# Seven block products in place of eight for some weight pairs of a feed-forward layer, in a fused attention and Fourier-mixing kernel

## The chip, the cores and the metric

The kernel runs on one core of one Trainium2 chip. The metric is the device time of one execution in microseconds (us), given as the median of several runs. One further execution was taken by the hardware profiler; all rows of the profile are from that one.

The engines are named as in the profile: PE (TensorE, matrix products; PEld is its weight load), DVE (VectorE), ACT (ScalarE), POOL (GpSimd) and SP (which here only issues DMAs).

## The reference

For 4 batches, 8 heads, 576 tokens and head size 64, an attention with a learned bias of the relative position gives x (4 x 576 x 512). Then a mixing block follows, all in float32:

```python
X = np.fft.fft(np.fft.fft(x, axis=1), axis=2)
u = x + np.real(X)
un = (u - mean(u)) / np.sqrt(var(u) + 1e-06)        # over the 512 features
ch = np.maximum(un @ w_ch1, 0.0) @ w_ch2            # 512 -> 2048 -> 512
return u + ch
```

The change concerns the product `un @ w_ch1` only.

## The kernel before

**Number format.** Every large product is made from float32r operands. A float32 value is split into a rounded high part and the rest as a low part (`split`: ACT copies the high part, POOL subtracts it to get the low part), and three products high x high, high x low, low x high are summed. `PROD = [(0, 0), (0, 1), (1, 0)]` lists them.

**Stages.** First the bias table is made, then attention runs over 16 units (4 head pairs x 4 batches); its order is written out by hand in the lists `SECOND`, `ORDER` and `TAIL`. The rest is the feed-forward part: four "dense batches" of 512 tokens (four tiles of 128), one for each batch, and a last one of 256 tokens which holds the 64 left-over tokens of all four batches (the "rest").

**A dense batch** (`dense`) runs over 16 feature blocks f of 128 hidden features. For each, `layer(f)` splits the block's first weight `w1[f]` (resident in SBUF, 128 x 512, four blocks of 128 input features), loads and splits the second weight `w2[f]`, makes the hidden features in `up(f)` and applies the ReLU and the split in `relu_parts(f)`. `up(f)` (L956) is 4 input blocks x 3 parts = 12 matmuls that move 512 tokens each. `down(f)` (L981) multiplies the hidden block into four output accumulators, one for each token tile: again 12 matmuls of 512 columns. `down(f-1)` is put behind `layer(f)`. `hps` has two PSUM banks for the results of `up`, `hhp` two buffers for the hidden parts, `wsp` two buffers for each kind of weight part. `end()` (L989) adds the accumulators into x and stores the tiles.

**What runs beside it.** While a batch's dense part runs, the next batch is made ready in small pieces (`prepare`): Fourier mixing (`Mix.pieces`: L652 to L718), mean and variance (L752), and scaling (L776), which writes the token tile `un`. `run` spreads these pieces over the batch's layers by weights written in the code. Then `flip` transposes `un` on PE (`across`, L797), and `high` (ACT, L802) and `low` (DVE, L806) make its two parts `uh` and `ul`, which the next batch's `up` reads. In batch 1, `widen_rest` also converts the last four weight blocks from 64-bit words.

**Order of the instructions.** In the dense part no order is written by hand: the framework lists each engine's instructions by priority (program order) and by its own estimate of when each is ready. Semaphores, buffer reuse and PSUM bank conflicts are handled by the framework.

Of the kernel before, what the change touches and what calls it, by code (L numbers as in the profile page):

```python
# [20 lines left out]
P = 128  # L21
# [109 lines left out]
def body(ctx, tc, a, out):  # L131
# [286 lines left out]
    with ExitStack() as st:  # L418
# [322 lines left out]

        def norm(tiles):
            n = len(tiles)
# [39 lines left out]
        def token_tile(name, n=4):  # L783

            if name not in toks:
                f = pp.tile([P, 2, 2, S], F32, tag="p", name=name, bufs=4)
                toks[name] = f.rearrange("p a b s -> p (a b s)")
            f = toks[name][:, :512 * n].rearrange("p (t d) -> p t d", d=512)
            return f if name == "un" else f.bitcast(F32R)

        def flip(un):
            ut, ps = [], {}

# [13 lines left out]

            return ut, across, high, low

# [3 lines left out]
        tl = [x[:, 0, t] for t in range(4)]  # L813
        un, stats, root, scale = norm(tl)
        ut, across, high, low = flip(un)
        col, w0 = {}, {}

# [75 lines left out]
        for w in TAIL:  # L893
# [12 lines left out]
            else:  # L906
                small[w[0]](*map(int, w[1:]))
        late.close()
        wsp = pool("wsp", 2, stack=st)
        fgp = pool("fgp", 1, stack=st)  # L910
# [16 lines left out]

        def dense(ut, tiles, store, n_first=0, mix=None):
# [6 lines left out]
            hs, w1s, w2s, wfs, hps_ = {}, {}, {}, {}, {}  # L935
            if n_first:
                hps_[0] = w0["ps"]

            def w1_parts(f):
                w1s[f] = split(w1[f], "w1", nc.gpsimd)  # L940

# [27 lines left out]
            def layer(f):  # L969
                if f not in w1s:  # L970
                    w1_parts(f)
# [12 lines left out]

            def end(which=None, parts=1):
# [19 lines left out]
            pieces = []  # L1005
            for f in range(n_first, NF):
# [57 lines left out]
        def prepare(tl, mix=None):  # L1064
# [4 lines left out]
            pcs += [(.65, lambda i=i: scale(i)) for i in range(n)]  # L1069
            ut, across, high, low = flip(un)  # L1070
# [6 lines left out]
            return tl, ut, pcs, [lambda t=t: one_tile(t) for t in range(n)]  # L1077

        rest_tiles = [x[:, 0, 4], x[:, 2, 4]]
        mix = Mix(1)  # L1080
        for b in range(B):
            def store(t, b=b):
                nc.sync.dma_start(out[4 * b + t], x[:, b, t])

            main, last_down, end = dense(ut, tl, store, 0 if b else 2, mix)
            if b + 1 < B:
                tl, ut, pcs, fl = prepare([x[:, b + 1, t] for t in range(4)], mix if b == 0 else Mix(b + 1))
            else:
                tl, ut, pcs, fl = prepare(rest_tiles)
            if b == 0:  # L1090
                run((main, 1.), (pcs, .94), (widen_rest(), .75))
            else:
                run((main, 1.), (pcs, .94))
            run((fl + last_down, 1.))
            end()

# [65 lines left out]
```

## Time and profile before

| what | us |
|---|---|
| median of 3 runs (lowest, highest) | 766.18 (766.15, 766.69) |
| the profiled execution, whole | 766.97 |
| its span, first to last instruction | 765.0 |
| PE busy in the span | 746.4 |
| DVE, ACT, POOL busy | 436.1, 432.1, 340.0 |
| dense batches 2, 3 and 4 together | 282.7 (433.37 to 716.10) |

The span is the time that the rows account for. The 2 us between it and the whole execution lie before the first and behind the last instruction. [...]

### The profile page before, as it was taken

How to read it: one execution, taken by the hardware profiler on the slowest of the kernel's cores; microseconds unless marked ns; L12 is line 12 of the kernel's file. 1: busy time of each engine (PE TensorE's matmuls, PEld its weight loads, DVE VectorE, ACT ScalarE, POOL GpSimd, SP SyncE). 2: the span in 40 equal slices, each digit the busy share in tenths (PEclk: the TensorE clock that was granted, in tenths of full speed). 3: DMA queues.
4: the chain of work that ended last, by engine and by line, in shares of the span. 5: the costliest groups of instructions: out<-in, count | busy, mean ns of one | idle time of the engine just before them, and what ended most of it. 6: DMA issues, size and time to landing. Idle time of an engine off the chain costs nothing.

```text
span 765.0 us, 13167 instructions
## 1 busy us (share of the span) xinstructions
PE 746.4 (98%) x4779; PEld 611.8 (80%) x4779; DVE 436.1 (57%) x958; ACT 432.1 (56%) x887; POOL 340.0 (44%) x291
## 2 busy tenths in 40 slices
PE   5899999999999999999999999999999999999998
PEld 3467887888878888878888888888888888888896
DVE  7997584887687888786665523334325331111443
ACT  7997887788888887843333433333333333333453
POOL 0002654754565654134554444544446444444442
PEclk9999999999999999999999999999999999999999
DMA  8988788679579872464421311113111222112332
GB/s 208 242 220 206 196 241 258 185 199 289 135 192 277 229 240 85 127 229 143 147 60 56 110 42 42 41 42 111 30 45 38 56 72 66 55 42 56 114 98 78
DMA packets 57584, 101.39 MB, mean 133 GB/s; under 512 B 8656, under 2 KB 27728, under 8 KB 56400
## 3 DMA queue, kind: packets, MB, share of 16 engines
q1 hardware_dynamic: 53792, 92.69, 43.2%
q10 hardware_dynamic: 3440, 4.78, 1.9%
q0 software_dynamic: 288, 3.08, 1.1%
q8 instruction: 37, 0.61, 0.3%
q14 instruction: 27, 0.22, 0.1%
HBM read 77.85 MB, written 20.02 MB: 128 GB/s over the span
## 4 chain that ended last, share of the span: by engine, by line
PE 91%; DVE 4%; DMA 2%; ACT 2%; issue 1%; SPq 0%; ACTq 0%; DVEq 0%
PE acc L981 26%; PE hp L956 25%; PE s L275 12%; PE o L475 10%; PE t L454 8%; PE bps L404 2%; PE zp L672 2%; PE abp L692 2%; DMA bias<-ring 1%; DVE hd L384 1%; PE t L444 1%; PE ut L797 1%; PE t L506 1%; DMA qT<-qT 1%; ACT ring L350 1%
## 5 line engine op out<-in xcount | busy, mean ns | idle before, releaser
L965 DVE SCALAR_TENSOR_TENSOR hl<-hp,hh 128x512 fp32r<-128x512 f32 (+1 forms) x80 | 51.0, 637 | 198.0 <-ACT hh L964 197.6
L925 POOL TENSOR_TENSOR w1l<-w,w1h 128x512 fp32r<-128x512 f32 x79 | 102.6, 1299 | 109.4 <-ACT w1h L924 107.1
L925 POOL TENSOR_TENSOR w2l<-w2f,w2h 128x512 fp32r<-128x512 f32 x64 | 84.8, 1325 | 106.9 <-ACT w2h L924 106.3
L296 DVE CUSTOM_DVE_ANT_0 p<-s,bias 128x576 f32<-128x576 f32 x128 | 95.2, 753 | 56.1 <-PE s L275 51.3
L956 PE MATMUL hp<-uh,w1l 128*128 128x512 f32 (+1 forms) x316 | 116.1, 368 | 0.0
L956 PE MATMUL hp<-uh,w1h 128*128 128x512 f32 (+1 forms) x316 | 116.0, 368 | 0.0
L924 ACT ACTIVATE w1h<-w 128x512 fp32r<-128x512 f32 x79 | 49.8, 631 | 114.2 <-PE hp L956 108.1
L956 PE MATMUL hp<-ul,w1h 128*128 128x512 f32 (+1 forms) x316 | 114.2, 368 | 0.0
L981 PE MATMUL acc<-w2h,hh 128*128 128x512 f32 x288 | 112.6, 392 | 0.0
L981 PE MATMUL acc<-w2l,hh 128*128 128x512 f32 x288 | 112.3, 390 | 0.0
L924 ACT ACTIVATE w2h<-w2f 128x512 fp32r<-128x512 f32 x80 | 50.5, 631 | 104.9 <-POOL w1l L925 54.6
L981 PE MATMUL acc<-w2h,hl 128*128 128x512 f32 x288 | 107.9, 391 | 0.0
L275 PE MATMUL s<-kh,qs 128*128 128x288 f32 (+1 forms) x320 | 98.3, 326 | 2.8 <-DVE nm L296 2.8
L434 ACT ACTIVATE pt<-t 128x512 f32<-128x512 f32 x141 | 77.8, 595 | 38.5 <-PE t L454 20.7
L311 ACT ACTIVATE p<-p,nm 128x576 f32<-128x576 f32 x128 | 98.2, 772 | 2.3 <-DVE nm L296 2.3
L275 PE MATMUL s<-kl,qs 128*128 128x288 f32 (+1 forms) x320 | 88.3, 295 | 0.9 <-DVE kl L216 0.9
L475 PE MATMUL o<-pt,v 128*64 128x288 f32 x640 | 84.2, 411 | 0.0
L212 POOL TENSOR_SCALAR kh<-kT 128x576 fp32r<-128x576 f32 (+1 forms) x28 | 21.0, 769 | 136.4 <-PE s L275 120.6
L454 PE MATMUL t<-ident,p 128*128 128x128 f32 x576 | 78.8, 273 | 0.6 <-ACT pt L434 0.6
L275 PEld LDWEIGHTS s<-kh,qs 128*128 128x128 f32 (+1 forms) x320 | 58.5, 183 | 19.1 <-issue 7.5
L475 PEld LDWEIGHTS o<-pt,v 128*64 128x64 f32 x640 | 43.3, 137 | 30.8 <-issue 4.7
L956 PEld LDWEIGHTS hp<-uh,w1h 128*128 128x128 f32 x316 | 59.5, 188 | 10.3
(154 smaller groups left out, 1391.6 us busy)
## 6 DMA issues: line engine op xcount, KB each, us to landing
w2f<-w_d SPq DMA_DIRECT2D x80, 256.0 KB, 2.7
raw<-m SPq DMA_DIRECT2D x24, 512.0 KB, 4.5
kT<-kT SPq DMA_DIRECT2D x32, 304.0 KB, 4.8
qT<-qT SPq DMA_DIRECT2D x32, 288.0 KB, 4.4
bias_d<-ring SPq DMA_DIRECT2D x54, 144.0 KB, 2.8
bias<-bias_d SPq DMA_DIRECT2D x24, 288.0 KB, 4.9
v<-v SPq DMA_DIRECT2D x16, 320.0 KB, 5.3
w_d<-wf SPq DMA_DIRECT2D x16, 256.0 KB, 3.5
```

What stands on the lines that cost most here:

```text
L212: nc.gpsimd.tensor_scalar(dst[:, c], src[:, c], 1.0, 0.0, ALU.mult, ALU.add)
L275: nc.tensor.matmul(ps[:m, c, :CH], qs[:, c0:c0 + m], kk[:, k0 + c * CH:k0 + (c + 1) * CH], start=k == 0, stop=k == 1, skip_group_check=True)
L296: nc.vector.tensor_tensor_reduce(p, bank.pop((n, i))[:, :, :CH], bias, -0.125, 3.0e38, ALU.add, ALU.min, nms[n][:, blk:blk + 1])
L311: nc.scalar.activation(p, p, AF.Exp, bias=nms[n][:, blk:blk + 1], scale=-1.0, accum_out=sums[n][:, blk:blk + 1])
L434: nc.scalar.activation(dst, src, AF.Copy)
L454: nc.tensor.transpose(tp[:, 128 * t:128 * t + 128], pb[t].rearrange("p h s -> p (h s)")[:, k0:k0 + 128], ident)
L475: nc.tensor.matmul(os_[u][e, c, :CH], vt[u][:, j, e], pts[u][:, 2 * j + h if j < 4 else 8, c * CH:(c + 1) * CH], start=j == 0, stop=j == 4 ...
L924: nc.scalar.activation(h, src, AF.Copy)
L925: eng.tensor_tensor(l, src, h.bitcast(F32), ALU.subtract)
L956: nc.tensor.matmul(ps[:, :N], w[wi][:, P * kb:P * kb + P], ut[ui][:, kb, :N], start=i == 0, stop=i == len(mm) - 1)
L965: nc.vector.scalar_tensor_tensor(hl[:, :N], ps[:, :N], 0.0, hh[:, :N].bitcast(F32), ALU.max, ALU.subtract)
L981: nc.tensor.matmul(acc[t], h[i][:, P * t:P * t + P], w[j], start=f == 0 and k == 0, stop=f == NF - 1 and k == 2)
```

## The change

For the last three pairs of feature blocks in dense batch 2, the last three in batch 3 and the last six in batch 4 (`START = [0, 5, 5, 2]`, 12 pairs in all), `up(2i)` and `up(2i+1)` are replaced by `pair(i)`. The pair is seen as a 2 x 2 block product: two feature blocks x two halves of the input features, times two halves of the input features x two halves of the tokens (256 each). Eight block products become seven, in the form with sums made ahead on both sides. Each is `product`: 2 input blocks x 3 parts = 6 matmuls that move 256 tokens. The remaining steps:

- `sums_(i)` makes four weight sums on DVE (128 x 256 each), `sum_parts` splits them, `own_parts` splits the plain blocks that are still needed.
- `keep` (ACT) writes the transposed tokens back in float32, into the tile that held the untransposed ones; `token_sums` makes four differences of them (DVE, in place) and splits them. It runs at a batch's begin.
- `one`, `two` and `three` issue 3 + 3 + 1 products and between them five additions of 128 x 256 on DVE and a copy on ACT. A pair takes both banks of `hps`.
- `paired` gives the order of a pair, with `down(f-2)` behind `one`, `down(f-1)` behind `two`, and the next pair's sums between. From the first pair of a batch to the end of that batch PE's order is as written.
- In these batches the preparation of the next one is spread over the layers before the first pair only (10, 10 and 4 layers).
- The normalised tokens of a following batch go to the tile named `raw`, which `widen_rest` also uses in batch 1.
- `dynamic_dma_scratch_size=4096` shrinks the SBUF area for the DMA descriptors that POOL makes; a new pool `sump` of 12 KB in each partition holds the sums' parts.

```diff
-                    un.append(token_tile("un", n))
+                    un.append(token_tile(name, n))
...
+            def keep(t):
+                nc.scalar.activation(un[0][:, t].rearrange("p (k c) -> p k c", c=P), ps[t], AF.Copy)
+            def token_sums():
+                b11, b12, b21, b22 = (un[0][:, i:i + 2, j:j + 256] for j in (0, 256) for i in (0, 2))
+                steps = [(b11, b12, b11), (b12, b22, b12), (b22, b22, b11), (b21, b21, b22)]
+                ts.append(token_tile("th"))
+                ts.append([rp.tile([P, 2, 512], F32R, tag="raw", name="tl") for rp in (rawp, rawd)])
+                def part(k, i, low):
+                    c = slice(256 * i, 256 * i + 256)
+                    src = un[0][:, 2 * i:2 * i + 2, 256 * k:256 * k + 256].rearrange("p t (k c) -> p t k c", c=P)
+                    h, l = (w.rearrange("p k (t c) -> p t k c", c=P) for w in (ts[0][:, 2 * k:2 * k + 2, c], ts[1][k][:, :, c]))
+                    if low:
+                        nc.vector.tensor_tensor(l, src, h.bitcast(F32), ALU.subtract)
+                    else:
+                        nc.scalar.activation(h, src, AF.Copy)
+                res = [(.8, lambda st=st: nc.vector.tensor_tensor(*st, ALU.subtract)) for st in steps]
+                res += [(.1, lambda w=w: part(*w, False)) for w in ((0, 0), (0, 1), (1, 1), (1, 0))]
+                return res + [(.9, lambda w=w: part(*w, True)) for w in ((0, 0), (0, 1), (1, 1), (1, 0))]
+            return ut, across, high, low, (ts, keep, token_sums)
...
+        def sums_(i):
+            f, g = w1[2 * i], w1[2 * i + 1]
+            sx, sy = (rp.tile([P, 512], F32, tag="wf", name="sum") for rp in (rawp, rawd))
+            for dst, one, two, op in (
+                    (sx[:, 0:256], g[:, 0:256], g[:, 256:512], ALU.add),
+                    (sx[:, 256:512], sx[:, 0:256], f[:, 0:256], ALU.subtract),
+                    (sy[:, 0:256], f[:, 0:256], g[:, 0:256], ALU.subtract),
+                    (sy[:, 256:512], f[:, 256:512], sx[:, 256:512], ALU.subtract)):
+                nc.vector.tensor_tensor(dst, one, two, op)
+            ss[i] = [sx, sy]
+        def sum_parts(i, k):
+            src = ss[i][k]
+            h = sump.tile([P, 512], F32R, tag=f"s{k}h", name=f"s{k}h")
+            l = sump.tile([P, 512], F32R, tag=f"s{k}l", name=f"s{k}l")
+            nc.scalar.activation(h, src, AF.Copy)
+            nc.gpsimd.tensor_tensor(l, src, h.bitcast(F32), ALU.subtract)
+            ss[i][k] = h, l
...
+        def own_parts(i):
+            w1_parts(2 * i)
+            src = w1[2 * i + 1][:, 256:512]
+            h = sump.tile([P, 256], F32R, tag="gh", name="gh")
+            l = sump.tile([P, 256], F32R, tag="gl", name="gl")
+            nc.scalar.activation(h, src, AF.Copy)
+            nc.gpsimd.tensor_tensor(l, src, h.bitcast(F32), ALU.subtract)
+            ss[i].append((h, l))
...
+            def product(dst, w, c0, block, first=False):
+                where, k, i = block
+                for kk in range(2):
+                    for wi, ui in PROD:
+                        if where == "u":
+                            src = ut[ui][:, 2 * k + kk]
+                        else:
+                            src = ts[1][k][:, kk] if ui else ts[0][:, 2 * k + kk]
+                        nc.tensor.matmul(
+                            dst, w[wi][:, c0 + P * kk:c0 + P * kk + P], src[:, 256 * i:256 * i + 256],
+                            start=first and kk == wi == ui == 0, stop=kk == 1 and wi == 1, skip_group_check=True)
+            def pair(i):
+                f, hold = 2 * i, {}
+                def one():
+                    x_, (sx, sy, g) = w1s.pop(f), ss.pop(i)
+                    pa, pb = (hps.tile([P, 512], F32, tag="h", name="hp") for _ in range(2))
+                    hold["w"] = x_, sy, g
+                    hold["p"] = pa, pb
+                    product(pa[:, 0:256], x_, 0, ("u", 0, 0), True)
+                    product(pa[:, 256:512], sx, 0, ("t", 0, 0))
+                    product(pb[:, 0:256], sx, 256, ("t", 1, 1), True)
+                    c = hold["c"] = sump.tile([P, 512], F32, tag="c", name="c")
+                    u2 = hold["u"] = toks["raw"][:, 2048:2304]
+                    nc.scalar.activation(c[:, 0:256], pa[:, 0:256], AF.Copy)
+                    nc.vector.tensor_tensor(c[:, 256:512], pa[:, 256:512], c[:, 0:256], ALU.add)
+                    nc.vector.tensor_tensor(u2, pb[:, 0:256], c[:, 0:256], ALU.add)
+                def two():
+                    (x_, sy, g), (pa, pb), c = hold["w"], hold["p"], hold["c"]
+                    product(pb[:, 0:256], sy, 0, ("t", 0, 1))
+                    product(pa[:, 0:256], x_, 256, ("u", 1, 0))
+                    product(pa[:, 256:512], sy, 256, ("u", 1, 1))
+                    nc.vector.tensor_tensor(c[:, 256:512], pb[:, 0:256], c[:, 256:512], ALU.add)
+                    nc.vector.tensor_tensor(pa[:, 256:512], pa[:, 256:512], hold["u"], ALU.add)
+                    hps_[f] = pa
+                    relu_parts(f)
+                def three():
+                    (x_, sy, g), (pa, pb), c = hold["w"], hold["p"], hold["c"]
+                    product(pb[:, 0:256], g, 0, ("t", 1, 0))
+                    nc.vector.tensor_tensor(c[:, 0:256], pb[:, 0:256], c[:, 0:256], ALU.add)
+                    hps_[f + 1] = c
+                    relu_parts(f + 1)
+                return one, two, three
+            def paired(p0):
+                res = []
+                for i in range(p0, NF // 2):
+                    f, (one, two, three) = 2 * i, pair(i)
+                    more = [(w1_parts, 0), (w1_parts, 1)]
+                    if i + 1 < NF // 2:
+                        more = [(sums_, i + 1), (sum_parts0, i + 1), (own_parts, i + 1), (sum_parts1, i + 1)]
+                    more = [(lambda m=m: m[0](m[1])) for m in more]
+                    res += [one] + more[:-3] + [lambda f=f: down(f - 2), lambda f=f: (w2_load(f), w2_parts(f)), two]
+                    res += more[-3:-2] + [lambda f=f: down(f - 1), lambda f=f: (w2_load(f + 1), w2_parts(f + 1))]
+                    res += more[-2:-1] + [three] + more[-1:]
+                return res
...
                 pieces.append(lambda f=f: layer(f))
-                if 0 < f < NF - 1:
+                if 0 < f < (2 * p0 if p0 else NF) - 1:
                     pieces.append(lambda f=f: down(f - 1))
+            if p0:
+                pieces = pieces, paired(p0)
...
+                if n == 4:
+                    keep(t)
...
+        START = [0, 5, 5, 2]
...
+            main, last_down, end = dense(ut, tl, store, 0 if b else 2, mix, ts, START[b])
+            first = token_sums() if b else []
...
+                run((fl + last_down, 1.))
+                end()
+                continue
+            i = START[b]
+            first = [(1.7, lambda: sums_(i)), (.1, lambda: sum_parts0(i)), (.1, lambda: sum_parts1(i))] + first
+            first += pcs + [(.1, lambda: own_parts(i))]
+            run((main[0], 1.), (first, .96))
+            with tc.manual_schedule(engines={PE_}):
+                for piece in main[1] + fl[:2] + last_down[:1] + fl[2:] + last_down[1:]:
+                    piece()
+                end()
...
-    nc = bacc.Bacc("TRN2", target_bir_lowering=False, num_devices=1)
+    nc = bacc.Bacc("TRN2", target_bir_lowering=False, num_devices=1, dynamic_dma_scratch_size=4096)
```

## Rows read from the trace of the kernel before

**Rows 1.** The page: span, busy time by engine, slices of the span.

```profile
span 765.0 us, 13167 instructions
PE 746.4 (98%) x4779; PEld 611.8 (80%) x4779; DVE 436.1 (57%) x958; ACT 432.1 (56%) x887; POOL 340.0 (44%) x291
PEclk9999999999999999999999999999999999999999
```

**Rows 2.** The page: the chain that ended last, by engine and line.

```profile
PE 91%; DVE 4%; DMA 2%; ACT 2%; issue 1%; SPq 0%; ACTq 0%; DVEq 0%
```

**Rows 3.** Stretches: length, busy us (instructions) of PE, PEld, DVE, ACT, POOL; clock.

```profile
433.37:716.10 282.73, 282.73 (x1318) 236.96 (x1318) 93.37 (x169) 98.89 (x182) 131.07 (x105) 1.00 0.20 56
649.93:660.81 10.88, 10.88 (x49) 9.01 (x49) 2.16 (x4) 3.50 (x7) 5.16 (x4) 1.00 0.18 48
628.01:644.30 16.29, 16.29 (x73) 13.51 (x72) 5.37 (x10) 5.25 (x9) 7.75 (x6) 1.00 0.38 114
```

**Rows 4.** The chain in order of time (start, us, what): batch 4, rest.

```profile
690.73 2.72 PE hp L956 x12
...
725.98 1.43 PE hp L956 x12
```

**Rows 5.** Weight loads and matmuls by shape, 725 to 757 us, the rest.

```profile
L956 PEld LDWEIGHTS hp<-uh,w1l 128*128 128x128 f32 x45 | 8.6, 191 | 0.0
...
L956 PE MATMUL hp<-ul,w1h 128*128 128x256 f32 x45 | 12.7, 283 | 0.0
```

**Rows 6.** DVE by shape, 343 to 765 us (busy us, mean ns).

```profile
L965 DVE SCALAR_TENSOR_TENSOR hl<-hp,hh 128x512 fp32r<-128x512 f32 x63 | 43.5, 690 | 185.2 <-ACT hh L964 184.9
...
L965 DVE SCALAR_TENSOR_TENSOR hl<-hp,hh 128x256 fp32r<-128x256 f32 x16 | 6.8, 424 | 12.7 <-ACT hh L964 12.7
```

**Rows 7.** DVE with both operands in SBUF: ns min/median/max, whole span.

```profile
L715 DVE TENSOR_TENSOR x<-x,dp x12: 408/660/871, 323.2 to 590.7; 128x255 f32<-128x255 f32 x8, 64x255 f32<-64x255 f32 x4
...
L664 DVE TENSOR_TENSOR gl<-ge,gh x8: 677/740/1776, 308.2 to 561.3; 128x512 fp32r<-128x512 f32 x8
```

**Rows 8.** ACT and POOL by shape, 343 to 765 us.

```profile
L924 ACT ACTIVATE w1h<-w 128x512 fp32r<-128x512 f32 x76 | 48.0, 631 | 114.2 <-PE hp L956 108.1 <-POOL w1l L925 4.3 <-POOL w2l L925 1.9
L964 ACT ACTIVATE hh<-hp 128x512 fp32r<-128x512 f32 x62 | 36.0, 581 | 6.2 <-PE hp L956 6.2
L802 ACT ACTIVATE uh<-ut 128x512 fp32r<-128x512 f32 x14 | 7.6, 598 | 3.4 <-PE ut L797 3.4
L964 ACT ACTIVATE hh<-hp 128x256 fp32r<-128x256 f32 x16 | 5.9, 368 | 2.4 <-PE hp L956 2.4
L660 ACT ACTIVATE gh<-ge 128x256 fp32r<-128x256 f32 x5 | 2.0, 408 | 2.5 <-DVE ge L656 2.5
...
L925 POOL TENSOR_TENSOR w1l<-w,w1h 128x512 fp32r<-128x512 f32 x77 | 100.0, 1299 | 100.2 <-ACT w1h L924 97.9 <-PE hp L956 2.2
L925 POOL TENSOR_TENSOR w2l<-w2f,w2h 128x512 fp32r<-128x512 f32 x63 | 83.5, 1325 | 104.5 <-ACT w2h L924 103.9 <-POOL x L718 0.5
```

**Rows 9.** Order of time, 723 to 727.5 us: DVE and POOL together.

```profile
723.39 1.30 POOL L925 TENSOR_TENSOR w1l<-w,w1h 128x512 fp32r<-128x512 f32 x1 [1.97 <-ACT w1h L924]
...
724.14 1.10 DVE L925 TENSOR_TENSOR w2l<-w2f,w2h 128x512 fp32r<-128x512 f32 x1
...
726.68 0.69 DVE L925 TENSOR_TENSOR w2l<-w2f,w2h 128x512 fp32r<-128x512 f32 x1 [0.75 <-ACT w2h L924]
```

**Rows 10.** POOL's second load: issue in the timeline, landing, its first reader.

```profile
308.00 0.60 POOL L610 DMA_DIRECT2D fd<-fd  x1 [3.82 <-DVE nm L296]
...
fd<-fd POOLq DMA_DIRECT2D x1, 1088.0 KB, 5.3
...
L692 PE MATMUL abp<-fd,z00h x4: 278/323/366, 319.4 to 321.9; 128*128 128x258 f32 x4
```

**Rows 11.** The tile `raw` in batch 1: last conversion, scaling behind it.

```profile
L169 DVE SCALAR_TENSOR_TENSOR wf<-wf,raw x16: 691/694/1069, 95.7 to 407.5; 128x512 int32<-128x512 int32 x16
...
L776 DVE TENSOR_SCALAR un<-x,mv,rs 128x512 f32<-128x512 f32 x4 | 2.1, 541 | 0.0
```

More of the change, by code (lines that the diff above doesn't have):

```diff
@@ L740, in pieces, with norm @@
                 return sum([feat(t) for t in range(2 + self.b % 2)], res)
-        def norm(tiles):
+        def norm(tiles, name="raw"):
             n = len(tiles)
@@ L788, in token_tile @@
             f = toks[name][:, :512 * n].rearrange("p (t d) -> p t d", d=512)
-            return f if name == "un" else f.bitcast(F32R)
+            return f if name in ("un", "raw") else f.bitcast(F32R)
         def flip(un):
-            ut, ps = [], {}
+            ut, ps, ts = [], {}, []
             def across(t, where):
@@ L908, in body @@
         late.close()
+        sump = pool("sump", 1, stack=st)
         wsp = pool("wsp", 2, stack=st)
@@ L926, in split, with w1_parts, sum_parts0, sum_parts1 @@
             return h, l
-        def dense(ut, tiles, store, n_first=0, mix=None):
+        w1s, ss = {}, {}
+        def w1_parts(f):
+            if f not in w1s:
+                w1s[f] = split(w1[f], "w1", nc.gpsimd)
+        def sums_(i):
[15 more added lines that the diff above has]
+            ss[i][k] = h, l
+        def sum_parts0(i):
+            sum_parts(i, 0)
+        def sum_parts1(i):
+            sum_parts(i, 1)
+        def w1_parts_(f):
+            return (0., lambda: w1_parts(f))
+        def own_parts(i):
[6 more added lines that the diff above has]
+            ss[i].append((h, l))
+        def dense(ut, tiles, store, n_first=0, mix=None, ts=None, p0=0):
             n = len(tiles)
@@ L1005, in dense @@
             pieces = []
-            for f in range(n_first, NF):
+            for f in range(n_first, 2 * p0 if p0 else NF):
                 pieces.append(lambda f=f: layer(f))
-                if 0 < f < NF - 1:
+                if 0 < f < (2 * p0 if p0 else NF) - 1:
                     pieces.append(lambda f=f: down(f - 1))
+            if p0:
+                pieces = pieces, paired(p0)
             if n == 2:
@@ L1069, in prepare @@
             pcs += [(.65, lambda i=i: scale(i)) for i in range(n)]
-            ut, across, high, low = flip(un)
+            ut, across, high, low, (ts, keep, token_sums) = flip(un)
             def one_tile(t):
@@ L1075, in one_tile @@
                 low(t)
-            return tl, ut, pcs, [lambda t=t: one_tile(t) for t in range(n)]
+                if n == 4:
+                    keep(t)
+            fl = [lambda t=t: one_tile(t) for t in range(n)]
+            return tl, ut, pcs, fl, ts, token_sums
         rest_tiles = [x[:, 0, 4], x[:, 2, 4]]
-        mix = Mix(1)
+        mix, ts, token_sums = Mix(1), None, None
+        START = [0, 5, 5, 2]
         for b in range(B):
@@ L1083, in store @@
                 nc.sync.dma_start(out[4 * b + t], x[:, b, t])
-            main, last_down, end = dense(ut, tl, store, 0 if b else 2, mix)
+            main, last_down, end = dense(ut, tl, store, 0 if b else 2, mix, ts, START[b])
+            first = token_sums() if b else []
             if b + 1 < B:
-                tl, ut, pcs, fl = prepare([x[:, b + 1, t] for t in range(4)], mix if b == 0 else Mix(b + 1))
+                tl, ut, pcs, fl, ts, token_sums = prepare(
+                    [x[:, b + 1, t] for t in range(4)], mix if b == 0 else Mix(b + 1))
             else:
-                tl, ut, pcs, fl = prepare(rest_tiles)
+                tl, ut, pcs, fl, ts, token_sums = prepare(rest_tiles)
             if b == 0:
                 run((main, 1.), (pcs, .94), (widen_rest(), .75))
[L1092 to L1095, printed above, removed]
+                run((fl + last_down, 1.))
[9 more added lines that the diff above has]
+                end()
         def store(t):
```

12 lines of the change are left out of this document (4 added, 8 removed).

## The prediction, made before the changed kernel was run

> **What bounds the kernel now.** [...] The chain that ended last is 91% PE [rows 2]. The change touches dense batches 2 to 4 only, so I then read the busy times of that stretch: from 433.37 to 716.10 us PE is busy in all of its 282.73 us, with DVE at a third, ACT at a third and POOL at less than half [rows 3]. So PE waits for nothing there. Work taken off PE is time won, until another engine comes late; work added to the others costs nothing until then. Two layers in the middle of batch 4 take 10.88 us for 48 matmuls, which is 0.2267 us for each matmul of 512 columns, and the twelve of one `up` are one piece of 2.72 us [rows 3, 4].
>
> **What comes off PE.** A pair had 24 `up` matmuls of 512 columns: 24 x 0.2267 = 5.44 us. It gets 42 of 256 columns. The kernel before has such matmuls, with the same operands and a weight load for each, in the rest: twelve in 1.43 us, 0.1192 each [rows 4]. 42 x 0.1192 = 5.01 us. A pair saves 0.435 us, twelve pairs 5.2 us. That is less than one eighth of the `up` time, since 256 columns cost a little more than half of 512. The `down` matmuls stay. The 0.1192 is the one price on which everything hangs, and it is measured; as a bound on the good side I take 0.118 (12 x 42 x 0.001 = 0.6 us more).
>
> [...]
>
> **What is added, and what hides it.** For one pair, in the 10.88 - 0.435 = 10.45 us that PE then needs for it:
>
> - DVE had two `hl` (0.690 each) [rows 6]. New are five additions of 256 columns with an operand in PSUM, 0.424 each by the 256-column `hl` [rows 6], 2.1 us together, and four weight sums with both operands in SBUF, each 0.408 us at best and 0.871 at worst by an operation of 255 columns [rows 7], 1.6 to 3.5 us. Sum: 5.1 to 7.0 of 10.45.
> - ACT splits three sum or weight tiles and two w2 tiles (5 x 0.631), half a tile (0.408), makes two ReLUs (2 x 0.581) and one copy from PSUM (0.368) [rows 8]: 5.1 of 10.45, against 3.50 in the two layers before [rows 3].
> - POOL subtracts three tiles of 1.299, half a tile (estimated at half, 0.65) and two of 1.325 [rows 8]: 7.2 of 10.45, against 5.16 [rows 3].
>
> None is full, so what counts is what is late for PE. PE's order in a pair is: `one` (18 matmuls, 2.15 us), `down` (2.72), `two` (2.15), `down` (2.72), `three` (0.72).
>
> The tightest wait that I find is the PSUM bank. A pair takes both banks of `hps`, so the next `one` can't write the first bank before `relu_parts(f)` has read it. From the end of `two` PE has a `down` and `three`, 3.44 us. In that time the matmul drains (duration 0.283 less pace 0.119: 0.16 [rows 5]), then follow an addition 0.424, the ReLU 0.581, `hl` 0.690 and some 0.1 for hand-overs: 2.0 us [rows 6, 8]. 1.4 us are left for whatever DVE or ACT has in front. The second bank is free after one addition, with 1.43 us of products before it is written. `two` needs the copy and two additions behind `one` (0.16 + 0.368 + 2 x 0.424 = 1.4 us), under a `down` of 2.72. The next pair's weight parts are needed a whole pair later; their single buffers (`s0`, `s1`, `gh`, `gl`) are free as soon as the step that reads them is over, which leaves several us for 0.631 on ACT and 1.299 on POOL. I cost these at nothing. Without the cover the bank would cost up to 2.0 us a pair.
>
> At a batch's begin `sums_` and `token_sums` come on top: eight DVE operations of 512 columns in SBUF at 0.677 us at best [rows 7] and 1.10 in a collision with POOL [rows 9], 5.4 to 8.8 us, and four sums, 1.6 to 3.5 us. Batches 2 and 3 have ten layers for that, over 45 us of PE. Batch 4 has six pieces of 2.72, 16.3 us, in which DVE was busy 5.37 and POOL 7.75 [rows 3]. DVE then has 12.4 to 17.7 us to do before the first pair, POOL 7.75 + 3 x 1.299 + 0.65 = 12.3. It fits at the lower end and is late by 1.4 us at the upper. The rest tiles' statistics and scaling slip into the pairs, where DVE has 3.4 us free in each.
>
> At the end of a batch, PE's fixed order puts eight transposes before each of the last two `down`. ACT has four `keep` more, 0.598 each by `high` [rows 8]. Two of them can lie between the last transposes and the next batch's first `up`: high, keep, high 1.8 us under a `down` of 2.72, hidden; uncovered it would be at most 0.6 us at each boundary.
>
> Further edits cost nothing. Scaled tokens go to `raw` in batch 1 only after the conversion's last use: the conversion's last step starts at 407.5, the four scalings lie between 410 and 425 [rows 11]. The smaller DMA area concerns POOL's two loads before the dense part; the tighter was issued at 308.0, lands in 5.3 us and is first read at 319.4 [rows 10], so some 5 us cover it. The 12 KB taken by `sump` equal the 12 KB given back by that area, so the buffers of the dense part need no other predecessor's memory.
>
> For what I can't see (the first bank at each start, where one ReLU and `hl`, about 1.5 us, stand against 1.43 us of products; batch 4's begin; now and then a DVE operation in front) I take 0.3 us for each batch and 0.3 for batch 4's begin: 1.2 us. Its bounds are 0 and 3.2 (the upper: an assumed 0.1 us in each pair, and at batch 4's begin the 1.4 above with one scaling of 0.541 [rows 11] in front).
>
> **Sum.** 766.97 us of the profiled execution - 5.2 + 1.2 = 763.0. That execution is 0.8 above the median of the runs, so on the median 766.18 I forecast 762.2, with its own range from 760.4 (no wait, 0.118) to 764.2.
>
> **Rivals.**
>
> *DVE and POOL take turns.* The trace has an instance: with POOL running from 723.39 to 724.69, the same DVE subtraction took 1.10 us that takes 0.69 alone, and it ended 0.55 us behind POOL's end [rows 9]. If all that DVE does with both operands in SBUF (four sums and one `hl`, 2.3 us a pair) has to lie outside POOL's 7.2, 9.5 of 10.45 us are taken, and an unlucky order makes the weight parts late. At the begin of batch 4 it is 8 x 0.677 + 4 x 0.408 = 7.0 beside 12.3 us, in 16.3: late by 3. Price: those 3 in place of 0.6, and up to 0.2 us in each pair: 2.4 to 4.8 more than the forecast, 764.2 to 767.0 or so, and the gain is eaten. Against it: the parts are needed late, and the instance cost DVE only what was left of POOL's operation. [...]
>
> *The bank decides (slower).* DVE's or ACT's queue in front of `relu_parts(f)` is longer than the 1.4 us left, in every pair. The point from which it decides is 1.4 + 0.435 = 1.84 us in front: two weight sums at 0.871 in the wrong place are 1.74. With 2.3 to 3 us in front the wait is 0.9 to 1.6 us a pair, 12 pairs lose 5 to 14 us net: 771 to 780. For it: instruction orders come from an estimate, and the sums stand in the program between `one` and `two`. Against: PE needs 2.72 us between these, in which the sums have their place.
>
> *Weight loads are not hidden (slower).* A load lasts 0.191 us in the rest [rows 5], longer than the pace of the matmuls there [rows 4]; a pair has 18 more. If they stood beside the matmuls the cost would be 12 x 18 x 0.191 = 41 us less the 5.2: 802. The pace of 0.1192 with a load for each speaks plainly against it. [...]
>
> *Something else moves.* The framework orders all instructions anew, also before 433 us, where POOL's area and the first stage's buffers lie elsewhere. I see no waiting there that this would end or make; a us or two either way.
>
> **How the numbers follow.** The forecast gets 0.62, turns of DVE and POOL 0.18, the bank 0.13, the loads 0.01, something else 0.06. Predicted: 762.2. The range for 8 in 10 reaches over the forecast and nearly all of the second case: 760.4 to 766.8. What a measurement here tells from no change is 0.2%, 1.5 us: faster is below 764.65, slower above 767.7. Faster: 0.62 + 0.05 of the second case + 0.03 of the last = 0.70. Same: 0.13 + 0.02 = 0.15. Slower: 0.13 + 0.01 + 0.01 = 0.15.
>
> **What the profile after would show.** Right: products in pieces of 2.15 and 0.72 us, PE without idle time from 433 to the end of batch 4, batches 2 to 4 shorter by 1.3, 1.3 and 2.6 us; PE busy down by about 5; POOL near 70% in the pairs. Turns: DVE's weight sums at 0.9 and more, `one` of the first pair of batch 4 waiting for DVE or POOL. Bank: PE idle before `one` in each pair, released by DVE at L965. Loads: products paced at 0.19 or more. I am wrong if the pace of the products isn't that of the rest, or if PE waits more than 0.4 us in each pair.

## The result, and the profile after

The change made the kernel slower: 778.27 us in the median of 4 runs (776.25 to 779.70) against 766.43 of the kernel before on the same chip; the ratio is 1.0143, with a 95% interval of 1.0124 to 1.0162. Forecast were 762.2 and a range of 760.4 to 766.8. The profiled execution took 778.17, its span 776.2.

First the page of the kernel after (span; busy time and count by engine; PE's clock in 40 slices; the chain that ended last):

```profile
span 776.2 us, 13843 instructions
PE 750.3 (97%) x4995; PEld 623.1 (80%) x4995; DVE 516.1 (66%) x1090; ACT 462.5 (60%) x947; POOL 372.5 (48%) x315
PEclk9999999999999999999999999999998998999999
PE 84%; DVE 9%; ACT 3%; DMA 2%; issue 1%; ACTq 0%; DVEq 0%; SPq 0%
```

Beside [rows 1, 2]: DVE's share of the chain has risen from 4 to 9% and PE's has fallen from 91 to 84%. PE is still busy 97%, so the loss must sit in a few places. The busy times by stretch name them. The first, third and fifth are what lies ahead of the first pair of batches 2, 3 and 4; the second, fourth and sixth are the pairs; then two stretches of 4 us behind waits (length; busy us and count of PE, PEld, DVE, ACT, POOL; clock):

```profile
432.95:492.45 59.50, 58.08 (x284) 49.36 (x283) 43.14 (x66) 25.25 (x48) 32.99 (x25) 1.00 0.21 62
492.45:522.84 30.39, 30.39 (x188) 27.44 (x189) 12.04 (x27) 12.68 (x23) 17.64 (x14) 1.00 0.15 45
530.09:597.15 67.06, 62.64 (x296) 52.64 (x295) 46.00 (x73) 25.14 (x53) 33.91 (x27) 0.95 0.17 55
597.15:627.53 30.38, 30.38 (x188) 27.43 (x189) 12.18 (x27) 12.76 (x24) 17.75 (x15) 1.00 0.14 44
634.60:656.24 21.64, 17.94 (x86) 14.90 (x84) 20.96 (x31) 10.21 (x20) 13.87 (x9) 0.98 0.28 95
656.24:720.89 64.65, 64.65 (x386) 58.20 (x387) 27.27 (x61) 27.91 (x49) 40.14 (x32) 0.95 0.16 46
...
589.90:593.90 4.00, 4.00 (x11) 3.10 (x10) 3.08 (x9) 0.73 (x2) 1.28 (x1) 0.50 0.00 0
656.30:660.30 4.00, 4.00 (x13) 3.42 (x14) 2.52 (x7) 0.63 (x1) 0.36 (x1) 0.50 0.01 2
```

In the pairs PE is busy throughout, as it was before [rows 3], and DVE, ACT and POOL have room. Ahead of them PE stands 1.42, 4.42 and 3.70 us, and DVE, which was busy a third of the time in these batches before, is busy 73%, 69% and 97%. And behind two of the waits the granted clock is 0.50.

The waits of PE from 430 us to the end (total, times, longest), all of them on `hl`, the low part of a hidden tile that DVE writes behind ACT's ReLU:

```profile
PE hp L1058 <- DVE hl L1030: 5.5, 3, 3.7
PE acc L1045 <- DVE hl L1030: 4.1, 2, 3.7
```

The chain in order of time (start, us, what): pieces of batch 2's pairs, then those behind the long waits of batches 3 and 4:

```profile
501.08 2.87 PE hp L1058 x24
503.96 2.75 PE acc L1045 x12
506.70 2.15 PE hp L1058 x18
...
511.60 2.87 PE hp L1058 x24
...
588.48 2.93 PE acc L1045 x6
591.41 3.77 PE hp L1021 x11
...
656.24 1.65 PE hp L1058 x6
657.88 4.80 PE acc L1045 x12
```

From 501.08 to 511.60 one pair passes in 10.52 us (the 24 products are `three` and the next `one`). The products have the pace forecast, 2.15 us for 18 (a product lasts 0.28 us in its row, the next starts 0.12 after it). At 588.48 six `down` matmuls take 2.93 us and at 657.88 twelve take 4.80. At the full clock twelve take 2.75 (503.96), and six half of that: this is the slow clock.

**The balance.** Waits 1.42 + 0.43 + 3.65 + 0.34 + 3.70 = 9.5 us. Slow clock, by the four pieces above against their own length at full clock: (2.93 - 1.36) + (3.77 - 11 x 0.2267) + (1.65 - 0.72) + (4.80 - 2.75) = 5.8 us. Pairs: 12 x (10.88 - 10.52) = 4.3 us won. 765.0 + 9.5 + 5.8 - 4.3 = 776.0, and the span is 776.2. That it fits to 0.2 us is partly luck: batch 2 begins 0.4 us earlier than before, and each wait costs some 0.2 us more than the profile gives it (worked out at run 12).

Who is in front of `hl`? The timeline of the kernel after, first in batch 3, then in batch 4 (start, us, engine, line, operation, tiles, count; in brackets the idle time before it and what ended it):

```profile
582.41 0.58 ACT L1029 ACTIVATE hh<-hp 128x512 fp32r<-128x512 f32 x1
...
584.49 0.48 DVE L704 SCALAR_TENSOR_TENSOR dm<-abp,dc,bs 128x257 f32<-128x257 f32 x1 [4.38 <-ACT bs L696]
...
585.40 1.52 DVE L715 TENSOR_TENSOR x<-x,dp 64x255 f32<-64x255 f32 x2
586.94 0.69 DVE L752 BATCH_NORM_STATS2 bn<-x 128x6 f32<-128x512 f32 x1
...
587.77 0.66 DVE L1030 SCALAR_TENSOR_TENSOR hl<-hp,hh 128x512 fp32r<-128x512 f32 x1
...
638.82 3.48 DVE L827 TENSOR_TENSOR raw<-raw 128x512 f32<-128x512 f32 x2
640.00 1.74 POOL L975 TENSOR_TENSOR s0l<-sum,s0h 128x512 fp32r<-128x512 f32 x1
641.71 1.74 POOL L975 TENSOR_TENSOR s1l<-sum,s1h 128x512 fp32r<-128x512 f32 x1
642.96 2.74 DVE L827 TENSOR_TENSOR raw<-raw 128x512 f32<-128x512 f32 x2
643.41 1.74 POOL L949 TENSOR_TENSOR w1l<-w,w1h 128x512 fp32r<-128x512 f32 x1
645.62 4.08 DVE L823 TENSOR_TENSOR tl<-raw,th 128x512 fp32r<-128x512 f32 x3
650.22 1.17 DVE L823 TENSOR_TENSOR tl<-raw,th 128x512 fp32r<-128x512 f32 x1
651.32 0.68 DVE L752 BATCH_NORM_STATS2 bn<-x 128x6 f32<-128x512 f32 x1
...
653.24 0.20 ACT L759 ACTIVATE rs<-rs 128x2 f32<-128x2 f32 x1 [4.17 <-DVE rs L758]
653.35 0.61 ACT L948 ACTIVATE w1h<-w 128x512 fp32r<-128x512 f32 x1
653.87 0.58 ACT L1029 ACTIVATE hh<-hp 128x512 fp32r<-128x512 f32 x1
654.27 1.31 DVE L776 TENSOR_SCALAR raw<-x,mv,rs 128x512 f32<-128x512 f32 x1
655.50 0.68 DVE L1030 SCALAR_TENSOR_TENSOR hl<-hp,hh 128x512 fp32r<-128x512 f32 x1
656.24 0.58 PE L1058 MATMUL hp<-th,s0h 128*128 128x256 f32 x1 [3.70 <-DVE hl L1030]
```

Batch 3: the ReLU's result `hh`, from which `hl` is made, is there at 582.99. DVE stands idle for 4.38 us in front of the mixing of the next tokens (`dm`), which waits for ACT's `bs`; then mixing and one tile's statistics go first, and `hl` behind them at 587.77. So DVE works through its list in order here, and the list holds a later batch's work ahead of the `hl` that PE needs. Batch 4: the eight token operations take 3.48 + 2.74 + 4.08 + 1.17 = 11.5 us. Then come the rest tiles' statistics; ACT waits 4.17 us with their square root (L759), and the split of a weight and the ReLU of the tile PE waits for stand behind it; then a scaling stands in front of `hl`.

The token differences by line (count; ns min/median/max):

```profile
L827 DVE TENSOR_TENSOR raw<-raw x12: 691/1670/1840, 437.3 to 644.0; 128x512 f32<-128x512 f32 x12
```

The median is 1.67 us against 0.69 alone; for their low parts (L823) it is 1.06 against 0.68. And POOL's subtractions next to them take 1.74 where [rows 8] give 1.30.

So there are three candidates ahead of the first pair: **the queue** (preparation is now listed ahead of the first pair, before `hl` and the ReLU), **collisions** of DVE and POOL (the longer operations of both), and **the first bank** (`one` takes both banks, so its second half waits for the ReLU and `hl` of the layer before under only 1.43 us of products). The pairs themselves are not one: PE is busy in all of their stretches.

### The profile page after: what moved, and what is told of

It is laid out like the page before. It is cut to its first block, busy times and chain, and to the rows that moved or that the text cites. A ratio compares the mean times of both kernels' runs of the same rounds, so it can differ in the third digit from the quotient of the medians.

```text
span 776.2 us, 13843 instructions
## 1 busy us (share of the span) xinstructions
PE 750.3 (97%) x4995; PEld 623.1 (80%) x4995; DVE 516.1 (66%) x1090; ACT 462.5 (60%) x947; POOL 372.5 (48%) x315
## 4 chain that ended last, share of the span: by engine, by line
PE 84%; DVE 9%; ACT 3%; DMA 2%; issue 1%; ACTq 0%; DVEq 0%; SPq 0%
PE acc L1045 24%; PE hp L1021 15%; PE s L275 11%; PE o L475 9%; PE t L454 7%; PE hp L1058 7%; PE bps L404 3%; PE zp L672 2%; PE abp L692 1%; DVE x L715 1%; DVE hl L1030 1%; DMA bias<-ring 1%; DVE bn L752 1%; PE t L444 1%; PE t L506 1%
## 5 line engine op out<-in xcount | busy, mean ns | idle before, releaser
L949 POOL TENSOR_TENSOR w2l<-w2f,w2h 128x512 fp32r<-128x512 f32 x64 | 87.6, 1369 | 90.0 <-ACT w2h L948 76.3
L949 POOL TENSOR_TENSOR w1l<-w,w1h 128x512 fp32r<-128x512 f32 x67 | 89.7, 1341 | 76.6 <-ACT w1h L948 72.0
L1021 PE MATMUL hp<-uh,w1l 128*128 128x512 f32 (+1 forms) x220 | 79.2, 360 | 0.0
L1021 PE MATMUL hp<-uh,w1h 128*128 128x512 f32 (+1 forms) x220 | 79.1, 360 | 0.0
L948 ACT ACTIVATE w1h<-w 128x512 fp32r<-128x512 f32 x67 | 42.1, 629 | 61.5 <-PE hp L1021 51.5
L1030 DVE SCALAR_TENSOR_TENSOR hl<-hp,hh 128x512 fp32r<-128x512 f32 (+1 forms) x68 | 42.4, 624 | 54.7 <-ACT hh L1029 54.3
L1021 PE MATMUL hp<-ul,w1h 128*128 128x512 f32 (+1 forms) x220 | 77.2, 360 | 0.0
L1045 PEld LDWEIGHTS acc<-w2h,hl 128*128 128x128 f32 x288 | 54.8, 192 | 16.5 <-DVE hl L1030 4.9
```

Source lines behind the costliest of these rows:

```text
L948: nc.scalar.activation(h, src, AF.Copy)
L949: eng.tensor_tensor(l, src, h.bitcast(F32), ALU.subtract)
L1021: nc.tensor.matmul(ps[:, :N], w[wi][:, P * kb:P * kb + P], ut[ui][:, kb, :N], start=i == 0, stop=i == len(mm) - 1)
L1030: nc.vector.scalar_tensor_tensor(hl[:, :N], ps[:, :N], 0.0, hh[:, :N].bitcast(F32), ALU.max, ALU.subtract)
L1045: nc.tensor.matmul(acc[t], h[i][:, P * t:P * t + P], w[j], start=f == 0 and k == 0, stop=f == NF - 1 and k == 2)
```

## Experiments

**1. The preparation spread over the whole batch again; only sums, token sums and the first parts ahead of the first pair.**

```diff
-            first += pcs + [(.1, lambda: own_parts(i))]
-            run((main[0], 1.), (first, .96))
+            first += [(.1, lambda: own_parts(i))]
+            run((main[0] + mark + main[1], 1.), (first, .96 * ahead_), (pcs, .94))
```

> The preparation of the next batch is spread over the whole batch again, as in the kernel before; only the weight and token sums stay ahead of the first pair. Theory 'queue' (the preparation was forced ahead of the first pair, and in DVE's fixed order the last hl of the plain layers stand behind it): the waits of 0.4 to 3.7 us before the first pairs of batches 2 and 3 go, batch 4's 3.7 shrink to under 2; 778 falls to 764 to 769. Theory 'load' (the token sums alone are too much for DVE): nothing changes before the first pairs, 775 to 779. Theory 'collisions' (POOL stretches DVE's operations): batch 4 keeps its wait, the others lose some; 770 to 775.

770.28 us (768.35 to 772.00, 7 runs), ratio 1.0041 [1.0020, 1.0062]: 8 of the 12 us come back. The waits behind mixing (3.65) are gone. Left are 1.18 us at batch 2's first pair, 2.38 at batch 4's with a slow stretch behind it (twelve `down` in 4.34 us), and 0.3 to 0.8 at three places in batch 3. At batch 2's, seven of the twelve products that should cover the ReLU and `hl` were drawn ahead of the last `up`, so little lay behind it. At batch 4's three of the token low parts (3.98 us, POOL beside them) still stand in front of `hl`.

**2. No token differences, and their low parts made by ACT as copies.**

```diff
-                        nc.vector.tensor_tensor(l, src, h.bitcast(F32), ALU.subtract)
+                        nc.scalar.activation(l, src, AF.Copy)
-                res = [(.8, lambda st=st: nc.vector.tensor_tensor(*st, ALU.subtract)) for st in steps]
-                res += [(.1, ...
+                res = [(.1, ...
```

> Left out: the four token differences on DVE; the token sums' low parts are plain copies on ACT. That takes 8 DVE operations of 0.7 to 1.8 us from each of batches 2 to 4. 'Load': all waits before the first pairs go, 764 to 767. 'Queue': batch 4's wait goes, since there the sums are most of DVE's work, but batch 3's 3.65 us behind the mixing chain stay; 769 to 773. 'Collisions': as load, since the collided operations are these.

770.87 us in one run. Against the expectation batch 3's 3.65 us is gone, and batch 4's wait stays with 2.72; the first bank's is 1.37 and 1.63 in batches 2 and 3. New are 1.20 and 1.21 us where batches 3 and 4 begin, behind `keep` on ACT. Batch 4's wait in this run (`hl` is L1029 here):

```profile
647.95 0.58 ACT L1028 ACTIVATE hh<-hp 128x512 fp32r<-128x512 f32 x1
...
650.95 0.68 DVE L1029 SCALAR_TENSOR_TENSOR hl<-hp,hh 128x512 fp32r<-128x512 f32 x1
```

The ReLU ends at 648.53, and until 650.95 DVE works on the rest tiles' root (for which it waits for ACT) and a scaling. No token operation is there; this wait is the queue's. Leaving operations out reorders the lists too, so the run does not separate queue and collisions in the kernel after; it shows that eight token operations fewer don't free the first pair of its wait.

**3. POOL quiet ahead of the first pair: the low parts made there are copied by ACT.**

```diff
-            eng.tensor_tensor(l, src, h.bitcast(F32), ALU.subtract)
+            if quiet:
+                nc.scalar.activation(l, src, AF.Copy)
+            else:
+                eng.tensor_tensor(l, src, h.bitcast(F32), ALU.subtract)
...
-            nc.gpsimd.tensor_tensor(l, src, h.bitcast(F32), ALU.subtract)
+            if quiet:
+                nc.scalar.activation(l, src, AF.Copy)
+            else:
+                nc.gpsimd.tensor_tensor(l, src, h.bitcast(F32), ALU.subtract)
```

> Left out: POOL's low parts of all weights made ahead of the first pairs in batches 2 to 4; ACT copies take their place. DVE's list is the same. 'Collisions': token differences and low parts at 0.69 each in place of 1.06 to 1.67, and no wait longer than 0.5 us: 764 to 768. 'Queue': the durations fall the same way, batch 4's wait falls from 3.7 to 0 to 1, but batch 3's wait behind the mixing chain stays above 2 us; 769 to 774. 'Load': as queue in batch 4.

770.75 us in one run. The token differences again:

```profile
L827 DVE TENSOR_TENSOR raw<-raw x12: 681/686/692, 436.5 to 642.3; 128x512 f32<-128x512 f32 x12
```

Every one has the length that it has alone, and so have their low parts (0.68). Batch 4's wait falls from 3.70 to 0.34, with DVE's operations in the same order as in the kernel after; the two in batch 3 behind mixing stay (0.96 and 2.74). So in that order batch 4's wait was the collisions', and batch 3's is the queue's. Run 2 shows that batch 4 has a wait from the queue as well when the list is another.

**4. Batch 4's first pair at layer 10** (nine pairs in all).

```diff
-        START = [0, 5, 5, 2]
+        START = [0, 5, 5, 5]
```

> Pairs in batch 4 from the sixth on, as in batches 2 and 3: three pairs fewer, 1.3 us more on PE, but 16 us more time before the first pair. All theories that put batch 4's wait on too little time for DVE: its 3.7 us and the slow stretch behind it (about 1.9) go, and the whole time is 772 to 775. A theory that the wait belongs to the switch into the pairs itself (two banks taken at once, whatever DVE does): 3 us or more of it stay, 778 to 780.

775.82 us in one run, 0.8 above the upper bound expected. Batch 4's wait falls to 1.76 and no slow stretch follows it (the next twelve `down` take 2.75 us); batches 2 and 3 are as after (1.43, 0.43, 3.65, 0.34). DVE is idle for 5.29 us in front of the `hl` that ends the 1.76, so these are the bank's. The dense batches also begin 2.15 us later here (435.10 against 432.95), before anything that the edit touches, so from there on the run won 4.5; why they begin later is open.

**5. As 1, and `down` ahead of the first `one`**, so that the bank has 2.75 us more.

```diff
-                    res += [(.8, one)] + more[:-3]
-                    res += [(1., lambda f=f: down(f - 2)), ...
+                    steps_ = [(.8, one)] + more[:-3], [(1., lambda f=f: down(f - 2))]
+                    res += steps_[1] + steps_[0] if i == p0 else steps_[0] + steps_[1]
```

> As e1_spread, and in the first pair of each batch the first down stands before the products of 'one', so that PE has 2.7 us more between the last plain up and the product that needs its bank. Theory 'queue and bank' (the last plain block's w1 split, ReLU and hl stand in a row before PE may write the second bank, with 1.43 us of cover): the waits of 1.18, 0.58 and 2.38 us before the first pairs go, and the slow clock of about 4 us behind the last with them; 770.3 falls by 5 to 6.5, to 764 to 765.5. Theory 'load' (DVE is full before the first pair whatever PE does): the waits move to the next product or down and stay, 769 to 771.

768.32 us (12 runs), ratio 1.0026 [1.0012, 1.0040]: better than 1, but a miss. The waits on the bank at the begins are gone, yet with the `down` moved away nothing lies between `one` and `two`, and `two` waits for its sum (`raw`, L1078) 1.83, 0.55 and 0.55 us, and behind the 1.83 the granted clock is 0.50 for 3.4 us (18 products take 3.02 us there and twelve `down` 3.70). I had moved the cover, not added one.

**6. As 5, with four pairs more in batches 2 and 3** (`START = [0, 3, 3, 2]`).

> As e5_down_first, with pairs from the fourth on in batches 2 and 3 (16 pairs in all, in place of 12). If a pair is worth 0.435 us and DVE's list has room: 1.7 us less than e5_down_first. 'Load': the shorter begin of batches 2 and 3 (six plain layers, with the mixing) brings waits of 1 us or more there, and the time is that of e5_down_first or above.

773.54 us (6 runs), ratio 1.0092 [1.0074, 1.0111]. New waits: PE's mixing matmuls (L672) stand 4.2 + 1.1 us for `gl` and `gh` from DVE. More pairs, at 0.36 each, cost more than they win as long as the next batch's preparation has to pass through the same engines.

**7. The kernel after, with only the `down` moved as in 5.**

> The changed kernel with that one move alone; the preparation stays ahead of the first pairs. 'Queue and bank': the waits at the first product of the second bank (1.42, 0.34 and 3.70 us) go or shrink to under 1 in batch 4, batch 3's 0.43 and 3.65 behind the mixing chain stay: 772 to 775. 'Load': nothing moves, 777 to 779.

769.56 us in one run, lower than expected. Batch 3's 0.43 and 3.65 stay to the hundredth, `raw` waits as in 5 (0.55, 0.52, 0.52), batch 4's wait is 1.02 in place of 3.70. The clock stays at its full level (1.000 in the mean of the execution), also behind the wait of 3.65, where twelve `up` matmuls take 2.74 us; so the 5.8 us of slow clock make up the larger part of the 8.7 that this run lies below the kernel after.

**8. As 5, with the moved `down` cut in two: half ahead of `one`, half behind it; batch 4 from layer 6** (eleven pairs).

```diff
+                    if i == p0:
+                        res.append((.5, lambda f=f: down(f - 2, [0, 1])))
                     res += [(.8, one)] + more[:-3]
-                    res.append((1., lambda f=f: down(f - 2)))
+                    res.append((1., lambda f=f, t=[2, 3] if i == p0 else None: down(f - 2, t)))
```

> As e1_spread, with the first pair's first down split: two tiles before 'one' and two behind it, so that PE has 1.36 us more in front of the second bank and keeps 1.36 us in front of 'two'; batch 4's pairs begin at the fourth (11 pairs). 'Queue and bank': the waits of e1_spread (1.18, 0.58, 2.38 us) and those that e5_down_first had at 'two' (1.83, 0.55, 0.55) are all under 0.5, only the 1.1 us in batch 3 behind the square root chain stay; against the kernel before 11 x 0.435 = 4.8 us of gain, less 1.1 to 2: 763 to 764. 'Load': other waits take their place, 766 to 769.

767.26 us (11 runs), ratio 1.0010 [0.9998, 1.0022]: the same as before, a miss by 3 us or more, and inside the range of 'load'. But 'load' has new waits in place of the old ones, and batch 4 is now free of waits; batch 2 keeps 0.46 and batch 3 five waits between 0.29 and 0.82 us. Batch 2's shows the first bank alone, first in the chain, then in the timeline of this run:

```profile
486.97 1.36 PE acc L1045 x6
...
488.45 2.08 PE hp L1021 x9
```

```profile
490.61 0.63 ACT L948 ACTIVATE w1h<-w 128x512 fp32r<-128x512 f32 x1 [3.37 <-PE hp L1021]
...
491.15 0.58 ACT L1029 ACTIVATE hh<-hp 128x512 fp32r<-128x512 f32 x1
...
491.76 0.69 DVE L1030 SCALAR_TENSOR_TENSOR hl<-hp,hh 128x512 fp32r<-128x512 f32 x1 [5.55 <-ACT hh L1029]
...
492.50 0.39 PE L1058 MATMUL hp<-th,s0h 128*128 128x256 f32 x1 [0.46 <-DVE hl L1030]
```

PE's list holds the half `down` (486.97) ahead of the last `up`'s rest (488.45), so only products lie behind that `up`. On ACT a weight's split goes first (490.61), the ReLU follows, then `hl`: from the end of `up` at 490.53 to 492.50 are 1.97 us, against some 1.5 of products. Nothing is late here, and the three operations have the lengths of [rows 6, 8]; the 0.46 is the bank's own price.

**9. As 8, with the four token low parts subtracted by POOL in place of DVE.**

> As e8_half_down, with the four low parts of the token sums on POOL in place of DVE. 'Collisions': DVE loses four operations of 0.7 to 1.8 us and what they wait for POOL; POOL gains four of about 1.3 per batch, serial with its own. If DVE's collisions still cost PE anything in e8_half_down, 0.5 to 1.5 us less than that; if not, the same time. If POOL comes late with the parts of the first pair: 1 to 3 us more, with waits for POOL at 'one'.

767.06 us (12 runs), ratio 1.0009 [0.9999, 1.0019], with the same waits to 0.1 us. In this arrangement it does not matter who makes these parts.

**10. As 8, with pairs in batch 4 alone** (five pairs; batches 2 and 3 run as in the kernel before).

```diff
-        START = [0, 5, 5, 3]
+        START = [0, 0, 0, 3]
```

> Pairs in batch 4 alone, from the fourth on (5 pairs), with the split down; batches 2 and 3 as in the kernel before, with no sums, no 'keep' for batches 2 and 3 and the preparation spread over the whole batch. The begin of batch 4 has no mixing beside it. Every theory: 5 x 0.435 = 2.2 us of gain if nothing waits: 764.4 against 766.6. If the time is 766 or more, something else than the waits that the trace names takes the gain, such as the new order in the stages before.

764.12 us (763.57 to 766.20, 8 runs), ratio 0.9971 [0.9958, 0.9984]: faster than both kernels. PE waits nowhere from 420 us to the end. Batch 4 from its first `up` to the transposes at its end, in the chain of the kernel before and then of this run:

```profile
628.17 5.44 PE hp L956 x24
...
709.77 0.87 PE ut L797 x8
```

```profile
626.99 5.44 PE hp L1021 x24
...
706.78 0.87 PE ut L797 x8
```

That is 81.60 us before and 79.79 now: five pairs win 1.81 us, 0.36 each. The two profiled executions differ by more, 766.97 - 764.03 = 2.9 us. The rest lies ahead of batch 2, which begins at 433.37 before and 1.2 us earlier, at 432.19, here. No run shows what made this, so not all of the 0.3% need be the pairs'.

**11 and 12. As 10, with batch 2's three pairs (11) or batch 3's three (12) added.**

> As e10_only_batch4, with batch 2's three pairs added again (five pairs of batch 4 and three of batch 2, batch 3 as in the kernel before). Theory, each batch pays for its own begin: in e8_half_down PE stood or ran slowly for 1.4 us more than its pace in batch 2 and 4.8 in batch 3. Then three pairs in batch 2 win 3 x 0.435 = 1.3 and lose 1.4, and the time is that of e10_only_batch4, 764.1 +- 0.6. Rival, the loss belongs to the first batch that starts pairs or to having them in several batches at all, and not to batch 3's mixing chain: then this run lies midway between e8_half_down and e10_only_batch4, 765.5 to 766, and so does the run with batches 3 and 4.

> As e10_only_batch4, with batch 3's three pairs added again (batch 2 as in the kernel before). Theory: batch 3's begin has the statistics chain of the next batch's tokens beside POOL's low parts and loses 4.8 where three pairs win 1.3: 764.1 + 3.5 = 767.6, between 766.5 and 768; waits of PE between 588 and 612 us, as in e8_half_down. Rival (loss belongs to several batches having pairs): 765.5 to 766 as in e11_batches_2_and_4.

11: 764.48 us (12 runs), ratio 0.9981 [0.9966, 0.9995]. 12: 767.00 us (12 runs), ratio 1.0008 [0.9996, 1.0021]. The theory's 764.1 and 767.6 hold, the rival's 765.5 to 766 for both does not: batch 2's pairs about pay for their begin, batch 3's lose 2.9 us. The rows agree: from its first `up` to the next batch's, batch 2 takes 96.65 us in run 10 and 96.43 in run 11, and batch 3 takes 98.15 in run 10 and 101.33 in run 12. PE has five waits in run 12, 0.58, 0.79, 0.34, 0.30 and 0.81 us, 2.8 together, three of them for `hl`. These numbers begin only where the last matmul ends, 0.28 us (256 columns) or 0.39 (512) after its start. From start to start, less the pace of two matmuls each, the five cost 4.1 us; three pairs win 1.1, which leaves 3.0 of the 3.2 us. The timeline of run 12 at the largest:

```profile
608.02 1.29 POOL L949 TENSOR_TENSOR w1l<-w,w1h 128x512 fp32r<-128x512 f32 x1
608.12 1.22 DVE L762 SCALAR_TENSOR_TENSOR rs<-rs 128x4 f32<-128x4 f32 x1
...
610.24 0.60 ACT L1029 ACTIVATE hh<-hp 128x512 fp32r<-128x512 f32 x1 [2.64 <-DVE hp L1086]
...
610.87 0.69 DVE L1030 SCALAR_TENSOR_TENSOR hl<-hp,hh 128x512 fp32r<-128x512 f32 x1 [0.67 <-ACT hh L1029]
...
611.70 0.35 PE L1058 MATMUL hp<-uh,w1h 128*128 128x256 f32 x1 [0.81 <-DVE hl L1030]
```

Here the bank does decide, in the middle of a pair: an operation of four elements in a row (the next batch's deviations) lasts until POOL's subtraction ends, 1.22 us, with the additions `c` and `hp`, the ReLU and `hl` queued behind it. Batch 3 has this because its pairs run beside the mixing and the statistics of batch 4's tokens.

## Why the prediction was wrong, step by step

- **The price of a pair: right in kind, 0.08 us too good.** The products have the pace of 0.1192 with a load each, 2.15 us for 18. A `down` between them takes 2.75 where I took 2.72; a pair takes 10.52, not 10.45. Twelve pairs win 4.3 us, not 5.2. (The 0.6 us of the good bound is 12 x 42 x 0.0012; the 0.001 printed there is too small.) Run 10's ratio (0.0029 x 767 = 2.2 us, interval 1.2 to 3.2) holds five of either price, 1.8 and 2.2; its rows decide for 0.36. To take the price from the kernel's own rows, 0.2267 and 0.1192, was right.
- **The engines' load in the pairs: right.** PE never stands in the twelve pairs of the kernel after; DVE is busy 12.0 of 30.4 us and POOL 17.6 (58%, below the 70% that I named). The bank rival, 0.13, does not occur there; it needs work of the next batch in DVE's list, as in run 12. Weight loads are hidden, as said: in batch 2's pairs they take 27.4 of 30.39 us, 0.19 each, and PE is idle in none of it.
- **The step that failed: the waits at the begins.** I put 1.2 us, with 3.2 as the upper bound. They are 9.5 us, and 5.8 for the slow clock behind them. The profiled execution came out 778.17 - 763.0 = 15.2 us above my sum: 15.3 - 1.2 = 14.1 of these are here, 0.9 are the pairs'. It failed in four places. "Batches 2 and 3 have ten layers for that, over 45 us of PE" reckons with an average, where DVE follows its list: in batch 3 it was idle for 4.38 us and then did other work first (run 1, which lists that work elsewhere, has no such wait; runs 3, 4 and 7, which leave the list, keep 2.7 to 3.65 of it). "The rest tiles' statistics and scaling slip into the pairs": they stood ahead of the first pair, with a square root in front of the ReLU on ACT. That "one ReLU and `hl`, about 1.5 us, stand against 1.43 us of products" leaves out the weight split of 0.63 us that ACT has in front; alone this costs 0.46 (the rows of run 8), and more where products are drawn ahead (run 1; 1.76 in run 4). And PE's full clock, 1.00 in [rows 3], was taken for given; behind two waits it was 0.50. Neither of the two signs of being wrong in the prediction's last sentence came: the products have their pace and PE doesn't wait within the pairs. Of the signs for turns, `one` of batch 4's first pair did wait for DVE, but the weight sums (L967) stayed at 0.41 to 0.43 in the median.
- **Turns of DVE and POOL: the effect right, the place right, the price too small.** The eight token operations of batch 4 took 11.5 us, above the bound of 8.8 that I made from the one collision in [rows 9], by 1.44 us for each in place of 1.10 at most. That rival's wait of 3 us for batch 4's begin was 3.70, and run 3 shows that it goes with POOL's work (0.34 us, the token differences at 0.69). How the two engines hold each other up is not shown, only how long their operations take. In batches 2 and 3 run 3 leaves the waits nearly as they were (1.37, 0.96, 2.74 and 0.34 against 1.42, 0.43, 3.65 and 0.34). The rival had no slow clock in its price. The lower end of its range is 762.2 + 2.4 = 764.6, not 764.2.
- **The causes don't add up one by one.** Each of runs 1, 2, 3 and 7 alone brings back 7.4 to 8.7 of the 11.8 us between the kernels, because each also has less of the slow clock: the kernel after has two stretches of 6.8 us, runs 1 and 3 one of 3.4 each, runs 2 and 7 none. Each of runs 2, 3 and 7 is one execution, so that part may be chance. So I give no share in us for queue, collisions and bank. That removing the remaining waits in batch 3 would give its three pairs' 1.1 us follows from run 12's sum; no run did it.

## What to carry to other kernels

Cost a rearrangement not by an engine's free share over a stage but by the list: which instructions stand ahead of the one that PE waits for, at the first place where the new stage begins. A scheme that trades matmuls for additions should start where no other preparation passes through the same engines; here the kernel with five pairs in the last full batch was faster by 0.3%, and the one with twelve, started beside the next batch's preparation, slower by 1.4%. When a transfer of cover is planned (a matmul group moved ahead of another), look at who lived under it before.

## What was not expected of the hardware

- An operation of four elements in a row was once as long as a large one: L762 took 1.22 us beside a POOL subtraction of 1.29 and ended with it (run 12, 609.34 and 609.31); in the kernel after, the line's five operations took 0.16 to 0.17.
- POOL loses too: 1.74 us in place of 1.30, three times in a row (640.00 to 643.41 above), when DVE's subtractions alternate with its own.
- The granted clock fell to 0.50 at PE waits of 3.65 and 3.70 us (kernel after, 6.8 us each time) and at 2.38 (run 1), 2.74 (run 3), 3.65 (run 4), 1.83 (run 5) and 3.02 (run 6), for 3.4 us each; in run 1 the `down` matmuls of that stretch start 0.43 us apart, otherwise 0.23. It did not at 2.72 (run 2) or 3.65 (run 7), both with a mean clock of 1.000. The seven executions of run 1 have mean clocks from 0.996 (772.00 us) to 1.000 (768.35), so the same kernel loses this time in some executions and not in others. What decides is open.
